# Seven products per pair of chunks: where the next pair's x is prepared, and when results are planted

## The chip, the core and the metric

One core of one Trainium2 chip runs the whole program: attention with landmarks, an MLP, a two-dimensional Fourier mix, a second MLP. The metric is the device time of one execution in microseconds (us); the core's engines are TensorE (PE, with its weight loads PEld), VectorE (DVE), ScalarE (ACT), GpSimd (POOL) and SyncE (SP), which issues the DMAs that matter here.

## The reference, cut to what matters

The change lies in the last stage: the second half of the second MLP.

```python
def _moe2_ref(x, w_ch1, w_ch2):
    X = np.fft.fft(x, axis=1)
    X = np.fft.fft(X, axis=2)
    mixed = np.real(X).astype(np.float32)
    u = x + mixed
    mu = np.mean(u, axis=-1, keepdims=True)
    var = np.mean((u - mu) ** 2, axis=-1, keepdims=True)
    un = (u - mu) / np.sqrt(var + 1e-06)
    ch = np.maximum(un @ w_ch1, 0.0) @ w_ch2
    return (u + ch).astype(np.float32)
```

`x` is 8 × 576 × 512, `w_ch1` 512 × 2048, `w_ch2` 2048 × 512, all float32.

## The kernel before, in words

The 4608 tokens are nine chunks of 512. Every float32 operand is kept as a high and a low part, and a product is three matmuls (high·high, low·high, high·low, each 128×128 times 128×512). The hidden 2048 columns are done in four quarters of 512; the last two are `quarters`, one pass over all chunks for each (`p` = 0, 1). A pass has five **units**: chunk 0 alone (the *single unit*), then four **pairs** of chunks. So there are ten units, numbered 0 to 9; 0 and 5 are the single ones.

In a pair the two chunks' up-projection is one 2 × 2 block product, made from seven block products instead of eight: sums and differences of blocks of x (`prepare`: `a` = x12 − x11, `b` = x22 − a, x12 ← x22 − x12, x21 ← x21 − b) meet blocks of weights that were combined beforehand, and partial sums in PSUM are copied on and added (`up_two`). The seven are the *roles* 0 to 6 of x: x11, a, b, x21, x12, x22, x21. The order of all work is written by hand: a unit is a list of **slots** (30 in a pair, 16 in a single unit), one slot is six matmuls of TensorE, `at(slot, fn)` files everything else. Each engine runs what it was given in the order of the slots, and within a slot in the order of filing: `up_two` or `up_one`, then `down`, then `prepare`, then loads.

- `up_two`, slots 0 to 13: two of the seven products' halves per role (lines 387 to 389). Line 494 (ACT) copies partial sums from bank to bank and the block s5 into SBUF; line 514 (DVE) makes the four **sums** (block c or b plus s5) in slots 8 to 11. `rectify`: line 455 (ACT) is the **Relu** into the high part of g, line 458 (DVE), a slot later, the **rest**, its low part.
- `down`, from slot 14 of a pair and slot 8 of a single unit: eight (four) result products of two slots each (lines 548 to 550). `get_res` (line 223, SP) fetches what earlier quarters left in DRAM, `plant` (line 539, ACT) copies it into the PSUM bank, where the product is added; only unit 0 adds it afterwards (line 555, DVE). The second pass also multiplies by a scale (559) and adds a skip (562). The four buffers `res` come free at the plant.
- `prepare` for the next unit, filed by this one: for each role `high` (line 421, ACT, the **cast**) and `low` (line 408, DVE, the **low**), and the **differences** (line 408, DVE too). Before, role r of a pair began in slot 2 + 3r, so 2, 5, 8, 11, 14, 17, 20.
- `load` (line 198, SP) for the unit after next: x11, x12, x22, x21 in slots 12, 22, 24, 27 of a pair; eight buffers `xf` in turn.

SP's queue is in order, and a DMA whose buffer is still read waits at its head. During the last pair of the first pass the eleven weights of the second pass (line 255, 512 KB each) pass through it too.

Of the kernel before, what the change touches and what calls it, by code (L numbers as in the profile page):

```python
# [34 lines left out]
def f32(ap):  # L35
    return ap.bitcast(F32)
# [3 lines left out]
def body(ctx: ExitStack, tc: tile.TileContext, qT, kT, vn, mU, mV, w11, w12, w21, w22,  # L40
# [146 lines left out]
    def rows(d):  # L187
        return slice(d * P, (d + 1) * P)
# [47 lines left out]
    class Mlp:  # L236
# [154 lines left out]
        def quarters(self, tail, ys, w1s, w2s, dst):  # L391
# [12 lines left out]
            def at(s, *fns):  # L404
                slots.add(s, [(0, fn) for fn in fns])

            def minus(out, a, b):
                nc.vector.tensor_tensor(out, a, b, op=ALU.subtract)

            def load(i, key):  # L410
                h, r = key
                c = units[i][1][h]
                ts = xin.setdefault(i, {})[key] = [self.pool.tile([P, NC], F32, name="xf", bufs=8) for _ in range(2)]
                for k in range(2):
                    un.get(c, 2 * r + k, ts[k])

            def high(i, r, k, src):
                n = 2 * r + k
                t = self.xtile(n)
                xs.setdefault(i, {})[r, k] = t  # L420
                nc.scalar.copy(t[:, 0, :], src())

            def low(i, r, k, src):
                t = xs[i][r, k]
                minus(t[:, 1, :], src(), f32(t[:, 0, :]))

            def prepare(i, s0, step):

                def X(h, r, k):
                    return lambda: xin[i][h, r][k]  # L430

                def sub(out, a, b):
                    return lambda: minus(out(), a(), b())

                pair = len(units[i][1]) == 2
                for k in range(2):
                    x11, x21 = X(0, 0, k), X(0, 1, k)
                    if pair:
                        x12, x22 = X(1, 0, k), X(1, 1, k)
                        a, b = (lambda k=k: t1[k]), (lambda k=k: t2[k])  # L440
                        pre = {1: [sub(a, x12, x11)], 2: [sub(b, x22, a)], 4: [sub(x12, x22, x12)], 6: [sub(x21, x21, b)]}
                        roles = (x11, a, b, x21, x12, x22, x21)
                    else:
                        pre = {2: [sub(x21, x21, x11)]}
                        roles = (x11, x21, x21)
                    for r, src in enumerate(roles):
                        s = s0 + step * r + k
                        at(max(s - 1, s0 + k) if r else s, *pre.get(r, ()))
                        at(s + 1, lambda r=r, k=k, src=src: high(i, r, k, src))
                        at(s + 2, lambda r=r, k=k, src=src: low(i, r, k, src))  # L450

            def rectify(g, key, src, s, wait=0):
                def relu():
# [64 lines left out]
            def down(i, s0, g):  # L518
                p, unit = units[i]
                seed = i > 0  # L520
                res, skip, sc, ps, out = {}, {}, {}, {}, {}
                outs = [(h, d) for h in reversed(range(len(unit))) for d in range(4)]

                def get_res(j, c, d):
                    res[j] = lp.tile([P, NC], F32, name="res", bufs=4)
                    ys[p].get(c, d, res[j])

                def get_skip(j, c, d):
                    skip[j] = lp.tile([P, NC], F32, name="skip", bufs=4)
                    tail[1].get(c, d, skip[j])  # L530

                def get_sc(c):
                    sc[c] = lp.tile([P, NC], F32, name="sc", bufs=2)
                    tail[0].get(c, sc[c])

                def plant(j):
                    ps[j] = self.bank8()
                    if seed:
                        nc.scalar.copy(ps[j], res[j])  # L539

                def mul(j, h, d, half):
                    w = self.w2[d]
                    ks = (2, 3, 0, 1) if h else (0, 1, 2, 3)
                    for k in ks[2 * half:2 * half + 2]:
                        gh, gl = g[h, k][:, 0, :], g[h, k][:, 1, :]
                        wh, wl = w[:, 0, rows(k)], w[:, 1, rows(k)]
                        first = not seed and k == ks[0]
                        nc.tensor.matmul(ps[j], wh, gh, start=first, stop=False, skip_group_check=True)  # L548
                        nc.tensor.matmul(ps[j], wl, gh, start=False, stop=False, skip_group_check=True)  # L549
                        nc.tensor.matmul(ps[j], wh, gl, start=False, stop=k == ks[3], skip_group_check=True)  # L550

                def take(j, c):
                    o = out[j] = lp.tile([P, NC], F32, name="out", bufs=3)
                    if not seed:
                        nc.vector.tensor_tensor(o, ps[j], res[j], op=ALU.add)
                    elif p == 0:
                        nc.scalar.copy(o, ps[j])
                    else:
                        nc.vector.tensor_tensor(o, ps[j], sc[c], op=ALU.mult)

                def add(j):
                    nc.vector.tensor_tensor(out[j], out[j], skip[j], op=ALU.add)

                def put(j, c, d):
                    dst[p].put(c, d, out[j])

                end = i + 1 == len(units)
                for j, (h, d) in enumerate(outs):
                    c, s = unit[h], s0 + 2 * j
                    lag = 0 if end and j + 1 == len(outs) else 1  # L570
                    at(max(s - 9, s0 - 8 + j), lambda j=j, c=c, d=d: get_res(j, c, d))
                    at(s - 3, lambda j=j: plant(j))
                    for half in range(2):
                        at(s + half, lambda j=j, h=h, d=d, half=half: mul(j, h, d, half))
                    at(s + 1, lambda j=j, c=c: take(j, c))
                    if p:
                        if d == 0:
                            at(s - 8, lambda c=c: get_sc(c))
                        at(max(s - 5, s0 - 6 + j), lambda j=j, c=c, d=d: get_skip(j, c, d))
                        at(s + 1 + lag, lambda j=j: add(j))  # L580
                    at(s + 1 + lag * (1 + p), lambda j=j, c=c, d=d: put(j, c, d))
# [14 lines left out]
            for i, (p, unit) in enumerate(units):  # L596
                s0, g, two = base[i], {}, len(unit) == 2
                last = unit == chunks[-1] and p == 0

                def begin(i=i, s0=s0, g=g, two=two, last=last):  # L600
                    (up_two if two else up_one)(i, s0, g)
                    down(i, s0 + (14 if two else 8), g)
                    if i + 1 < len(units):
                        prepare(i + 1, s0 + (2 if two or i else 6), 3 if two else 2)
                    if i + 2 < len(units):
                        for key, s in (((0, 0), 12), ((1, 0), 22), ((1, 1), 24), ((0, 1), 27)):
                            if key[0] < len(units[i + 2][1]):
                                at(s0 + (s if two else max(s - 12, 6)), lambda key=key: load(i + 2, key))
                    if last:
                        for n in range(7):  # L610
                            at(s0 + 2 * n + 3, lambda n=n: (self.w1.append(0), self.w1.pop(), self.fetch("w1", w1s[n])))
                        for d in range(4):
                            at(s0 + 24 + 2 * d, lambda d=d: self.fetch("w2", w2s[d]))
                for s in range(s0, s0 + lens[i]):
                    if s == s0:
                        if i and units[i - 1][0] != p:
                            self.w1, self.w2 = self.w1[7:], self.w2[4:]
                        begin()
                    slots.run(s)
                    yield 1  # L620
# [817 lines left out]
```

## Time and profile before

| | us |
|---|---|
| median of three runs | 1900.45 (1896.96 to 1901.38) |
| the profiled execution: time / span | 1895.0 / 1893.2 |
| TensorE busy | 1838.3 |
| VectorE / ScalarE / GpSimd busy | 1018.3 / 705.9 / 373.6 |
| mean granted clock of TensorE | 0.995 |

The span is from the first to the last instruction of the profiled execution. Times in the trace are us from its start. Busy time is a mean over stages, so each stage has to be looked at by itself. A wait is put down to the instruction that came last before it ended.

### The profile page before, as it was taken

Reading aid. Unit: us, or ns where it says so; the run is one execution under the profiler, and the core shown is the slowest. Engines: PE = TensorE matmul, PEld = TensorE weight load, DVE = VectorE, ACT = ScalarE, POOL = GpSimd, SP = SyncE. Lnnn points to the kernel's source line nnn. Section 1 sums busy time; section 2 is a strip of 40 time slices with the busy share of each in tenths; the row PEclk is TensorE's granted clock in tenths of the full one; section 3 lists DMA queues with packets and bytes.
Section 4 is the critical chain, followed back from the end, with each engine's and each line's share of the span. In section 5 each row is a group of like instructions: output and inputs, shape, how many; then the busy total and the mean of one; then the engine's idle time right before and its main releaser. Section 6 shows DMA issues by size and latency. Waiting matters only on the chain.

```text
span 1893.2 us, 30600 instructions
## 1 busy us (share of the span) xinstructions
PE 1838.3 (97%) x12088; PEld 1484.4 (78%) x12088; DVE 1018.3 (54%) x1764; ACT 705.9 (37%) x1469; POOL 373.6 (20%) x352
## 2 busy tenths in 40 slices
PE   6989999999999999999999999999999999999998
PEld 5767777777788888887887888888888877777777
DVE  7886556555323334755645455474332364438764
ACT  3544443444212212323333243343322365546442
POOL 2333211221201221313222043232321000000000
PEclk9999999999999999999999999999999999999999
DMA  7444445442537333524536554243533555476665
GB/s 262 143 171 159 146 165 199 140 154 99 179 126 272 126 130 117 171 95 156 191 106 244 173 178 160 90 155 120 164 104 113 178 178 150 134 250 207 207 188 156
DMA packets 175391, 305.56 MB, mean 161 GB/s; under 512 B 27440, under 2 KB 92560, under 8 KB 175248
## 3 DMA queue, kind: packets, MB, share of 16 engines
q1 hardware_dynamic: 170640, 294.17, 46.7%
q10 hardware_dynamic: 4608, 9.44, 1.3%
q8 instruction: 95, 1.56, 0.3%
q14 instruction: 48, 0.39, 0.1%
HBM read 195.74 MB, written 107.22 MB: 160 GB/s over the span
## 4 chain that ended last, share of the span: by engine, by line
PE 86%; DVE 7%; ACT 3%; DMA 3%; issue 1%; SPq 0%; ACTq 0%; POOL 0%; DVEq 0%
PE ps L348 10%; PE ps L350 10%; PE ps L349 10%; PE ps L299 10%; PE ps L301 9%; PE ps L300 9%; PE ps L548 4%; PE ps L550 3%; PE ps L549 3%; PE ps L389 2%; PE ps L388 2%; PE ps L387 2%; PE ps_f L76 1%; PE ps_f L77 1%; PE ps_f L78 1%
## 5 line engine op out<-in xcount | busy, mean ns | idle before, releaser
L299 PE MATMUL ps<-x,w 128*128 128x512 f32 x864 | 345.5, 400 | 0.0
L348 PE MATMUL ps<-g,w 128*128 128x512 f32 x864 | 345.4, 400 | 0.0
L350 PE MATMUL ps<-g,w 128*128 128x512 f32 x864 | 337.5, 391 | 0.9 <-DVE g L304 0.7
L301 PE MATMUL ps<-x,w 128*128 128x512 f32 x864 | 337.4, 390 | 0.0
L349 PE MATMUL ps<-g,w 128*128 128x512 f32 x864 | 337.0, 390 | 0.0
L300 PE MATMUL ps<-x,w 128*128 128x512 f32 x864 | 336.9, 390 | 0.0
L304 DVE SCALAR_TENSOR_TENSOR g<-ps,g 128x512 fp32r<-128x512 f32 x216 | 148.8, 690 | 333.0 <-ACT g L303 332.3
L303 ACT ACTIVATE g<-ps 128x512 fp32r<-128x512 f32 x216 | 128.9, 597 | 374.5 <-PE ps L301 373.8
L348 PEld LDWEIGHTS ps<-g,w 128*128 128x128 f32 x864 | 162.1, 188 | 39.2 <-issue 5.3
L350 PEld LDWEIGHTS ps<-g,w 128*128 128x128 f32 x864 | 162.2, 188 | 37.0 <-DVE g L304 2.1
L301 PEld LDWEIGHTS ps<-x,w 128*128 128x128 f32 x864 | 162.1, 188 | 35.1
L299 PEld LDWEIGHTS ps<-x,w 128*128 128x128 f32 x864 | 162.2, 188 | 34.4
L300 PEld LDWEIGHTS ps<-x,w 128*128 128x128 f32 x864 | 162.5, 188 | 31.6
L349 PEld LDWEIGHTS ps<-g,w 128*128 128x128 f32 x864 | 162.4, 188 | 31.5
L104 POOL TENSOR_TENSOR cvp<-cvp,cva 128x512 f32<-128x512 f32 x56 | 72.7, 1299 | 383.8 <-DVE cvp L103 383.8
L548 PE MATMUL ps<-g,w 128*128 128x512 f32 x288 | 115.6, 402 | 14.2 <-ACT ps L539 14.2
L358 DVE TENSOR_TENSOR xf<-ps,xf 128x512 f32<-128x512 f32 x76 | 52.4, 689 | 123.0 <-PE ps L350 121.0
L550 PE MATMUL ps<-g,w 128*128 128x512 f32 x288 | 114.8, 399 | 0.3 <-DVE g L458 0.3
L549 PE MATMUL ps<-g,w 128*128 128x512 f32 x288 | 114.8, 398 | 0.0
L52 POOL TENSOR_TENSOR x<-xf,x 128x512 fp32r<-128x512 f32 (+7 forms) x56 | 67.6, 1211 | 237.2 <-ACT x L51 218.3
L548 PEld LDWEIGHTS ps<-g,w 128*128 128x128 f32 x288 | 55.6, 193 | 29.5 <-ACT ps L539 17.9
L52 POOL TENSOR_TENSOR stg<-cva,stg 128x512 fp32r<-128x512 f32 x40 | 57.3, 1432 | 72.0 <-ACT stg L51 71.6
(350 smaller groups left out, 2886.5 us busy)
## 6 DMA issues: line engine op xcount, KB each, us to landing
d<-stg SPq DMA_DIRECT2D x54, 512.0 KB
w<-d SPq DMA_DIRECT2D x54, 512.0 KB
wraw<-w SPq DMA_DIRECT2D x48, 512.0 KB
y<-xf SPq DMA_DIRECT2D x76, 256.0 KB
res<-y SPq DMA_DIRECT2D x72, 256.0 KB
xf<-y SPq DMA_DIRECT2D x40, 256.0 KB
u<-u1T ACTq DMA_DIRECT2D x32, 288.0 KB
U<-x SPq DMA_DIRECT2D x8, 1152.0 KB
```

The lines of the kernel that those rows point to most:

```text
L52: (eng or nc.vector).tensor_tensor(lo, src, f32(hi), op=ALU.subtract)
L299: nc.tensor.matmul(ps, wh, xh, start=k == 0, stop=False)
L300: nc.tensor.matmul(ps, wl, xh, start=False, stop=False)
L301: nc.tensor.matmul(ps, wh, xl, start=False, stop=k == 3)
L303: nc.scalar.activation(g[:, 0, :], ps, AF.Relu)
L304: nc.vector.scalar_tensor_tensor(out=g[:, 1, :], in0=ps, scalar=0.0, in1=f32(g[:, 0, :]), op0=ALU.max, op1=ALU.subtract)
L348: nc.tensor.matmul(ps, wh, gh, start=k == m0, stop=False)
L349: nc.tensor.matmul(ps, wl, gh, start=False, stop=False)
L350: nc.tensor.matmul(ps, wh, gl, start=False, stop=k == m1 - 1)
L548: nc.tensor.matmul(ps[j], wh, gh, start=first, stop=False, skip_group_check=True)
L549: nc.tensor.matmul(ps[j], wl, gh, start=False, stop=False, skip_group_check=True)
L550: nc.tensor.matmul(ps[j], wh, gl, start=False, stop=k == ks[3], skip_group_check=True)
```

## The change

The slots of the preparation become a list: in a pair the roles begin in 2, 4, 13, 16, 19, 22, 25, so that no role lies in slots 8 to 13; the differences are filed behind the low of the role before. Results are planted at `s - 4` instead of `s - 3` and fetched at `s - 10` instead of `s - 9`. The loads stand in slots 10, 24, 27, 29 of a pair. The single units have lists of their own.

```diff
@@ def prepare @@
-            def prepare(i, s0, step):
+            def prepare(i, s0, starts):
...
-                        pre = {1: [sub(a, x12, x11)], 2: [sub(b, x22, a)], 4: [sub(x12, x22, x12)], 6: [sub(x21, x21, b)]}
+                        pre = {0: [sub(a, x12, x11)], 1: [sub(b, x22, a)], 3: [sub(x12, x22, x12)], 5: [sub(x21, x21, b)]}
                         roles = (x11, a, b, x21, x12, x22, x21)
                     else:
-                        pre = {2: [sub(x21, x21, x11)]}
+                        pre = {1: [sub(x21, x21, x11)]}
                         roles = (x11, x21, x21)
                     for r, src in enumerate(roles):
-                        s = s0 + step * r + k
-                        at(max(s - 1, s0 + k) if r else s, *pre.get(r, ()))
+                        s = s0 + starts[r] + k
                         at(s + 1, lambda r=r, k=k, src=src: high(i, r, k, src))
-                        at(s + 2, lambda r=r, k=k, src=src: low(i, r, k, src))
+                        at(s + 2, lambda r=r, k=k, src=src: low(i, r, k, src), *pre.get(r, ()))
@@ def down @@
-                    at(max(s - 9, s0 - 8 + j), lambda j=j, c=c, d=d: get_res(j, c, d))
-                    at(s - 3, lambda j=j: plant(j))
+                    at(max(s - 10, s0 - 8 + j), lambda j=j, c=c, d=d: get_res(j, c, d))
+                    at(s - 4, lambda j=j: plant(j))
@@ def quarters @@
-                        prepare(i + 1, s0 + (2 if two or i else 6), 3 if two else 2)
+                        prepare(i + 1, s0, (2, 4, 13, 16, 19, 22, 25) if two else range(2, 16, 2) if i else range(7, 21, 2))
                     if i + 2 < len(units):
-                        for key, s in (((0, 0), 12), ((1, 0), 22), ((1, 1), 24), ((0, 1), 27)):
+                        for key, s in (((0, 0), 10), ((1, 0), 24), ((1, 1), 27), ((0, 1), 29)):
+                            if not two:
+                                s = {10: 8, 24: 14, 27: 17, 29: 19}[s] + (5 if i == 0 else 0)
                             if key[0] < len(units[i + 2][1]):
-                                at(s0 + (s if two else max(s - 12, 6)), lambda key=key: load(i + 2, key))
+                                at(s0 + s, lambda key=key: load(i + 2, key))
```

The changed file has one line less above `rectify`, so its lines from there to the lists of loads are numbered one lower than before (457 for 458, 513 for 514, 538 for 539).

VectorE's queue in a pair, from the first sum to the last (w_14139 is the sum, w_14136 s5, w_14137 the block a, w_14138 the block b; ps is a PSUM bank). Before:

```order
L514 TENSOR_TENSOR w_14139<-ps,w_14136 128x512
L458 SCALAR_TENSOR_TENSOR g<-ps_14739,g 128x512
L408 TENSOR_TENSOR x<-w_14137,x 128x512
L408 TENSOR_TENSOR w_14138<-xf,w_14137 128x512
L458 SCALAR_TENSOR_TENSOR g<-w_14139,g 128x512
L514 TENSOR_TENSOR w_14139<-ps,w_14136 128x512
L514 TENSOR_TENSOR w_14139<-ps_14748,w_14136 128x512
L458 SCALAR_TENSOR_TENSOR g<-w_14139,g 128x512
L408 TENSOR_TENSOR xs<-w_14138,xs 128x512
L458 SCALAR_TENSOR_TENSOR g<-w_14139,g 128x512
L514 TENSOR_TENSOR w_14139<-ps_14749,w_14136 128x512
```

The same place in the change:

```order
L513 TENSOR_TENSOR w_14139<-ps,w_14136 128x512
L457 SCALAR_TENSOR_TENSOR g<-ps_14739,g 128x512
L457 SCALAR_TENSOR_TENSOR g<-w_14139,g 128x512
L513 TENSOR_TENSOR w_14139<-ps,w_14136 128x512
L513 TENSOR_TENSOR w_14139<-ps_14748,w_14136 128x512
L457 SCALAR_TENSOR_TENSOR g<-w_14139,g 128x512 x2
L513 TENSOR_TENSOR w_14139<-ps_14749,w_14136 128x512
L457 SCALAR_TENSOR_TENSOR g<-w_14139,g 128x512
```

The two lows and the difference that stood between the sums are gone from there.

ScalarE's queue in the single unit of the second pass, from its first two Relus on (the third Relu makes the first half of what the second of the unit's result slots reads). Before:

```order
L455 ACTIVATE g<-ps 128x512 x2
L421 CAST x<-xf 128x512 x2
L455 ACTIVATE g<-ps 128x512
L539 COPY ps_15842<-res 128x512
L421 CAST x<-w_14137 128x512 x2
L455 ACTIVATE g<-ps_15853 128x512
L539 COPY ps_15878<-res 128x512
```

In the change:

```order
L454 ACTIVATE g<-ps 128x512 x2
L421 CAST x<-xf 128x512
L538 COPY ps_15829<-res 128x512
L421 CAST x<-xf 128x512
L454 ACTIVATE g<-ps 128x512
L421 CAST x<-w_14137 128x512
L538 COPY ps_15859<-res 128x512
L421 CAST x<-w_14137 128x512
L454 ACTIVATE g<-ps_15852 128x512
```

The first plant has moved past one cast and the third Relu, the second past a cast and the fourth Relu.

SP's queue at the end of the pair ahead of that unit (w is a weight of the second pass, y a result written, xf a load of x in pieces of two batches, res the first result that the single unit plants). Before:

```order
L255 DMA w_15742<-d_19_172 128x1024
L198 DMA xf<-un_183 128x64
L198 DMA xf<-un_184 128x448
L198 DMA xf<-un_183 128x64
L198 DMA xf<-un_184 128x448
L226 DMA y_7_103<-out 128x512
L255 DMA w_15765<-d_20_173 128x1024
L226 DMA y_7_103<-out 128x512
L255 DMA w_15776<-d_21_174 128x1024
L223 DMA res<-y_0_96 128x512
```

In the change:

```order
L226 DMA y_7_103<-out 128x512
L255 DMA w_15759<-d_20_173 128x1024
L198 DMA xf<-un_183 128x64
L198 DMA xf<-un_184 128x448
L198 DMA xf<-un_183 128x64
L198 DMA xf<-un_184 128x448
L226 DMA y_7_103<-out 128x512
L255 DMA w_15776<-d_21_174 128x1024
L223 DMA res<-y_0_96 128x512
```

The last load of x has moved behind one more weight and one more written result, next to the first fetch of a result.

## Rows read from the trace of the kernel before

**Rows 1.** The page, busy time: engine, us, share of the span, instructions.

```profile
PE 1838.3 (97%) x12088; PEld 1484.4 (78%) x12088; DVE 1018.3 (54%) x1764; ACT 705.9 (37%) x1469; POOL 373.6 (20%) x352
```

**Rows 2.** TensorE in order of time: start, us, line, tiles [idle before, releaser].

```profile
1494.63 0.39 PE L387 MATMUL ps<-x,w 128*128 128x512 f32 x1
...
1505.29 0.39 PE L389 MATMUL ps<-xs,w 128*128 128x512 f32 x1
...
1537.58 0.63 PE L548 MATMUL ps<-g,w 128*128 128x512 f32 x1 [1.99 <-ACT ps L539]
...
1693.56 0.39 PE L387 MATMUL ps<-x,w 128*128 128x512 f32 x1
...
1707.58 0.50 PE L550 MATMUL ps<-g,w 128*128 128x512 f32 x1 [0.30 <-DVE g L458]
...
1888.21 0.39 PE L550 MATMUL ps<-g,w 128*128 128x512 f32 x1
```

**Rows 3.** Waits from 1494.6 to 1893.2: us in total, times, longest.

```profile
PE ps L548 <- ACT ps L539: 14.2, 8, 2.1
...
PE ps L550 <- DVE g L458: 0.3, 1, 0.3
```

**Rows 4.** Busy time, granted clock (PEclk), DMA share and GB/s behind two waits.

```profile
1537.60:1541.30 3.70, 3.70 (x9) 2.91 (x10) 3.39 (x7) 2.48 (x5) 0.00 (x0) 0.54 0.40 104
1582.20:1585.90 3.70, 3.70 (x16) 3.09 (x17) 3.39 (x7) 3.15 (x7) 0.00 (x0) 1.00 0.46 110
```

**Rows 5.** VectorE in order of time, unit 0 and the first pair.

```profile
1508.94 0.69 DVE L555 TENSOR_TENSOR out<-ps,res 128x512 f32<-128x512 f32 x1 [0.65 <-DMA res<-y]
...
1523.78 0.69 DVE L408 TENSOR_TENSOR w<-xf 128x512 f32<-128x512 f32 x1
...
1529.49 0.69 DVE L514 TENSOR_TENSOR w<-ps,w 128x512 f32<-128x512 f32 x1 [0.86 <-ACT ps L494]
1530.10 0.68 DVE L458 SCALAR_TENSOR_TENSOR g<-ps,g 128x512 fp32r<-128x512 f32 x1
...
1531.90 0.68 DVE L458 SCALAR_TENSOR_TENSOR g<-w,g 128x512 fp32r<-128x512 f32 x1
...
1535.69 0.68 DVE L514 TENSOR_TENSOR w<-ps,w 128x512 f32<-128x512 f32 x1
```

**Rows 6.** ScalarE in order of time, the first pair.

```profile
1530.22 0.63 ACT L455 ACTIVATE g<-w 128x512 fp32r<-128x512 f32 x1 [0.76 <-DVE w L514]
...
1536.41 0.63 ACT L455 ACTIVATE g<-w 128x512 fp32r<-128x512 f32 x1 [1.01 <-DVE w L514]
1536.95 0.58 ACT L539 COPY ps<-res 128x512 f32<-128x512 f32 x1
```

**Rows 7.** SP's own waits, 1494 to 1893: total, times, longest.

```profile
SPq L198 <- DVE xs L408: 18.0, 7, 7.1
```

**Rows 8.** SP's queue in order of time: start, us, line, tiles, DMAs.

```profile
1518.80 2.00 SPq L198 DMA_DIRECT2D xf<-un  x4
...
1683.95 1.83 SPq L198 DMA_DIRECT2D xf<-un  x4
...
1696.90 0.51 SPq L223 DMA_DIRECT2D res<-y  x1
...
1866.47 0.32 SPq L223 DMA_DIRECT2D res<-y  x1
```

**Rows 9.** ScalarE in order of time: two plants that waited for their result.

```profile
1703.85 0.59 ACT L539 COPY ps<-res 128x512 f32<-128x512 f32 x1 [1.33 <-DMA res<-y]
...
1869.82 0.59 ACT L539 COPY ps<-res 128x512 f32<-128x512 f32 x1 [0.84 <-DMA res<-y]
```

**Rows 10.** As rows 4, up to the first result of the second pass.

```profile
1684.00:1692.00 8.00, 8.00 (x37) 6.60 (x37) 0.00 (x0) 2.75 (x6) 0.00 (x0) 1.00 0.80 221
1692.00:1704.00 12.00, 12.00 (x55) 9.93 (x54) 4.99 (x8) 3.56 (x7) 0.00 (x0) 1.00 1.02 379
```

**Rows 11.** The page, DMA issues: queue, times, KB each.

```profile
w<-d SPq DMA_DIRECT2D x54, 512.0 KB
...
res<-y SPq DMA_DIRECT2D x72, 256.0 KB
```

## The prediction

> **What bounds the kernel now.** I first read the page's head: TensorE is busy for 97% of the span [rows 1], so time is to be won only where it stands or runs slowly. Then I took TensorE's instructions in order of time, and who waits for whom, in the part that the change touches. The diff touches only `quarters`, which runs from the first product of line 387 at 1494.63 to the last of line 550 at 1888.21 [rows 2]. It issues 1632 products (256 on each of lines 387 to 389, 288 on each of 548 to 550). The first 47 steps from one to the next take 10.66 us, from 1494.63 to 1505.29, so a step is 0.2268 us, and a slot of six 1.361 us. 1631 such steps are 369.9 us; the stretch is 393.6 us long. So **23.7 us** is all that can be won.
>
> Where they are: TensorE waited 14.2 us in eight waits on line 548 for ScalarE's line 539, and 0.3 us once for VectorE [rows 3]. The eight are the eight pair units, at the same place: the first result product (slot 14) stands until its planted result is there. Seven last 1.93 to 2.06 us, as at 1537.58 [rows 2]; the last pair, which prepares nothing, waits 0.32. From start to start each is 0.16 longer than its idle time, so the eight are 15.5 us. After four of them the granted clock went to its lower level, 1.2 GHz: 0.54 on average in the 3.7 us behind the first, with nine products done, while it was 1.00 behind the second, with sixteen [rows 4]. Such a stretch costs seven steps of 0.2268, 1.6 us, four of them 6.5. The rest is 0.6 in the single unit of the second pass, where line 550 at 1707.58 should by the same count have started at 1706.94 (1693.56 and 59 steps), and about 1 in steps of 0.1.
>
> Why ScalarE is late: in the first pair (its slot 14 is due at 1535.46, 30 slots after 1494.63) VectorE starts the first sum at 1529.49 and the last at 1535.69 [rows 5]; three of the instructions that stand between them are line 408, the preparation. The last Relu waits for that last sum and the plant stands behind this Relu in ScalarE's queue: 1536.41, 1536.95, ending 1537.53 [rows 6].
>
> **The change, part by part.** No instruction is added or dropped; all terms are waits.
>
> 1. *Preparation out of slots 8 to 13.* Between the first and the last sum VectorE's queue now holds rests and sums alone. I walk it with the spacings of the rows (0.60 for VectorE, 0.53 for ScalarE). Sum at 1529.49, rest 1530.10, first Relu of a sum 1530.22 as before [rows 6], done 1530.85; its rest 1530.9 instead of 1531.90 [rows 5]; the next two sums 1531.5 and 1532.1; their Relus 1532.2 and 1532.75.
>
> 2. *Plant a slot sooner.* It stands now behind the third Relu, not the fourth: start 1533.3, end 1533.9. Due at 1535.46, it has 1.6 us to spare. The third and second rests follow (1532.85, 1533.45), the fourth sum at 1534.05, its Relu at 1534.8, its rest at 1535.45, done at 1536.1; this one is due a slot after the plant, at 1536.8. So the wait goes in all seven, and in the last pair, 0.48 from start to start, too. The low stretches of the pairs all stood behind such waits and go with them: **15.5 + 6.5 + 1 = 23 us** go. The moved work fits: slots 4 to 7 get nine VectorE instructions of 0.60, 5.4 us of the 5.4 that four slots last, and the slots from 8 on, two each, are under 1.36.
>
> 3. *Loads behind the last use.* SP is one queue in order, and a load put before its buffer is free holds up all behind it: 18.0 us in seven waits, up to 7.1 [rows 7]. Now it doesn't stand there. Its price is less time from load to use: for x12 from 12 slots to 10, 13.6 us; for x22 from 13 to 9, 12.2 us. A transfer of 256 KB in a quiet stretch is ready 3.35 us after its issue (1866.47 to 1869.82 [rows 8, 9]); in the worst one that the rows show 6.95 (1696.90 to 1703.85 [rows 8, 9]). I count nothing. Bounds: none at 6.95; 0.5 for x12 if a wait of SP of 7.1 came before that as well (14.05 against 13.6).
>  In the first pair the distance is shortest: the load of x12 now stands in slot 19, its first use in slot 20. By VectorE's queue, 18 instructions after 1508.94 [rows 5] x12 is read for the last time, so the load starts at 1520.5 (1518.80 before [rows 8]); with 3.35 for its second half, issued 0.5 later, it is there at 1524.3. VectorE gets to its first reader 25 instructions after 1508.94, at 1524.0 (1523.78 before [rows 5]). 0.3 us of lateness against the 1.6 of point 2: nothing. With 6.95 it would be a wait of about 2 and a stretch of low clock, 0 to 3.7 us.
>
> 4. *The single unit of the second pass.* Here something new is late. Before, ScalarE stood until 1703.85 for the first result from DRAM [rows 9], but the Relu for half the next slot was already done. Planted a slot sooner, the plant stands **ahead** of one cast of x, of that Relu and of what they feed. Walked from the landing P: cast P+0.53, Relu P+1.05; then VectorE, in its new order, low, difference, rest, low, difference, low, difference, rest: eight at 0.60 from P+1.2, the last over at P+6.1. The last product of slot 9 needs that last rest. At the same landing this is 1709.95 instead of 1707.58, 2.4 us later. And the landing moves: the loads ahead of it start two slots (2.72 us) later, from the 1683.95 of before [rows 8], into DMA queues which were 0.80 busy for 8 us and then full, 1.02, up to the landing [rows 10]. At most 1.6 us of the 2.72 can be made good (0.20 of 8); I take half, 0.8, so the landing is 1.9 late. Sum 4.3 us, with 0.6 of before 4.9; and since four waits in seven of about 2 us brought the low clock, 1.6 more: **6.5 us** lost here. Bounds: 0 (three loads and four weights of 512 KB, four results of 256 KB and its own [rows 11] are 4.75 MB, at 379 GB/s [rows 10] 12.5 us; so it would land before its plant is due) to 7.4 (all of 2.72, and the low clock).
>
> Sum: 23.7 − 6.5 = **17.2 us**. The profiled execution took 1895.0, so 1877.8; it lies 5.45 under the median of 1900.45, from which the forecast goes: **1883 us**. A measurement of this kernel can tell some 0.3%, 5.7 us, from no change.
>
> **Rivals.** (a) *The single unit loses nothing*, since SP, no longer held up for the late plants of the pair before it, is through sooner. For: SP's loads stood in such waits [rows 7]. Against: the DMA queues, not SP, were full from 1692 on [rows 10]. 1900.45 − 23.7 + 0.6 = 1877.
>
> (b) *Pairs wait for DMA instead.* The plant is asked for at 1533.3, its result is issued in slot 6 of the pair, 1524.6: 8.7 us, a slot less than before, and a ScalarE that stands there holds the Relu behind it. Against: 6.95 was the worst landing. Two or three pairs at 2.1 + 1.6 give back 7 to 11 us: 1890 to 1894, with the first pair's wait of point 3 in the same sum.
>
> (c) *Slower: the later loads become the bound.* VectorE meets the first reader of x12 in slot 4, with the sums of slot 8 queued behind it. From 13.6 + 1.6 = 15.2 us after the issue on, each us of landing is one us of wait, in seven pairs, with 1.6 of low clock each. It must eat 17.2 + 5.7 = 23 us, so 3.3 per pair: landings of 17 us. Against: 6.95 is the longest in the rows; for: in the second pass the loads now stand within six slots, beside what the results move. It would give 1906 to 1915. The Trainium skill, "DMA: Bandwidth & Descriptors", section "Rules for kernel authors", says to issue a DMA early and wait for it late, which speaks for this rival; the trace agrees only so far as the buffer is free, since a load issued before that made SP stand up to 7.1 us [rows 7].
>
> (d) *No change*: the wait at slot 14 comes back from another side, say the fourth Relu's rest. Point 2 leaves it 0.7 us of room. 1900.
>
> **Chances.** Forecast 50% (own range 1879 to 1888: point 4 with at least 2 of its loss, points 3 and 4 at their upper bounds), (a) 25%, (b) 16%, (c) 4%, (d) 5%. (b) is faster by over 5.7 us in nearly all of its range; so faster 0.91, same 0.05, slower 0.04. The range leaves out (c), (d) and the upper end of (b), and reaches below (a) by the 3 us by which the runs of before spread under their median: 1874 to 1891.
>
> **What would show it.** Right: no wait of line 547 (548 before) for the plant in the eight pairs; clock 1.00 throughout them; rests and sums side by side on VectorE; in the single unit a wait of 2 us or more between its slots 8 and 10, ended by the plant or by VectorE. Wrong: waits of about 2 us still at slot 14, then the VectorE queue was not the cause; ScalarE standing for results from DRAM in the pairs, then (b); VectorE standing for x, then (c).

## The result and the profile after

The changed kernel takes **1878.86 us** (median of four runs, 1875.06 to 1879.98); the kernel before took 1898.70 beside it (four runs, 1896.90 to 1901.38). The ratio is 0.9891, with a 95% interval of 0.9870 to 0.9912: 19.8 us less. The forecast was 1883, range 1874 to 1891. Unrounded it was 1900.45 − 17.2 = 1883.25; of the 4.4 us between, 1.75 are the median of before, which a fourth run moved from 1900.45 to 1898.70, and 2.6 are one term of the sum.

The page of after, its busy line (all of after's lines behind `prepare` carry a number one lower than before's):

```profile
PE 1838.0 (98%) x12088; PEld 1486.0 (79%) x12088; DVE 1020.0 (54%) x1764; ACT 707.6 (38%) x1469; POOL 374.1 (20%) x352
```

Over the whole span the busy times are those of [rows 1] within 2 us. In the part that the diff touches TensorE's is not: the same products take longer at the lower clock. From the first product of line 387 on, before and after (busy time of each engine, then granted clock, DMA share and GB/s):

```profile
1494.63:1888.60 393.97, 379.47 (x1633) 309.90 (x1631) 228.71 (x362) 194.93 (x355) 0.00 (x0) 0.98 0.60 187
1499.38:1873.60 374.22, 371.54 (x1633) 305.81 (x1631) 230.66 (x362) 195.58 (x355) 0.00 (x0) 1.00 0.63 197
```

Of the gain there, 11.8 us are idle time that is gone (14.5 to 2.7), and 7.9 are busy time (379.5 to 371.5). TensorE's waits in the part (us in total, times, longest), against the 14.2 in eight of [rows 3]:

```profile
PE ps L549 <- DVE g L457: 2.0, 2, 1.7
PE ps L547 <- ACT ps L538: 0.5, 1, 0.5
```

These three are in the single unit of the second pass. No pair waits for its plant any more, and the granted clock stays at 1.00 behind every first result product of a pair.

A total needs care here. The code ahead of `quarters` is the same in all kernels, yet the first product of line 387 comes at 1494.63 in the profile of before and between 1496.57 and 1501.22 in the other nine. So I compare this **part** by itself, from the first product of line 387 to the last of line 549 (550): 393.58 us before, 373.81 after (1499.38 to 1873.19). The steps alone need 369.9; 23.7 us of excess have become 3.9. That saves 19.8, as the medians do.

**A pair after the change.** VectorE in the second pair, slots 8 to 12 (start, us, line, tiles):

```profile
1575.29 0.69 DVE L513 TENSOR_TENSOR w<-ps,w 128x512 f32<-128x512 f32 x1 [0.39 <-ACT ps L493]
1575.90 0.68 DVE L457 SCALAR_TENSOR_TENSOR g<-ps,g 128x512 fp32r<-128x512 f32 x1
1576.68 0.69 DVE L457 SCALAR_TENSOR_TENSOR g<-w,g 128x512 fp32r<-128x512 f32 x1
1577.29 1.28 DVE L513 TENSOR_TENSOR w<-ps,w 128x512 f32<-128x512 f32 x2
1578.67 1.29 DVE L457 SCALAR_TENSOR_TENSOR g<-w,g 128x512 fp32r<-128x512 f32 x2
1579.88 0.68 DVE L513 TENSOR_TENSOR w<-ps,w 128x512 f32<-128x512 f32 x1
```

Four sums and four rests, and no line 408 between them. The same pair on ScalarE (the second and third Relu of a sum, then the plant), and its first result product on TensorE:

```profile
1578.01 1.23 ACT L454 ACTIVATE g<-w 128x512 fp32r<-128x512 f32 x2 [0.88 <-DVE w L513]
1579.14 0.58 ACT L538 COPY ps<-res 128x512 f32<-128x512 f32 x1
```

```profile
1581.29 0.39 PE L547 MATMUL ps<-g,w 128*128 128x512 f32 x1
```

The plant stands behind three Relus, not four, and ends at 1579.72, 1.57 us before it is needed. Point 2 gave it 1.6.

**The single unit of the second pass**, where 3.7 of the 3.9 us are. Its first product is at 1684.65. SP issues the fetch of its first result, ScalarE plants it, VectorE makes what follows, TensorE waits three times:

```profile
1690.08 0.45 SPq L223 DMA_DIRECT2D res<-y  x1
```

```profile
1695.58 0.59 ACT L538 COPY ps<-res 128x512 f32<-128x512 f32 x1 [4.18 <-DMA res<-y]
1696.10 0.61 ACT L421 CAST x<-xf 128x512 fp32r<-128x512 f32 x1
1696.62 0.59 ACT L454 ACTIVATE g<-ps 128x512 fp32r<-128x512 f32 x1
```

```profile
1696.75 0.69 DVE L408 TENSOR_TENSOR x<-xf,x 128x512 fp32r<-128x512 f32 x1 [3.94 <-ACT x L421]
...
1700.96 0.68 DVE L457 SCALAR_TENSOR_TENSOR g<-ps,g 128x512 fp32r<-128x512 f32 x1
```

```profile
1696.22 0.50 PE L547 MATMUL ps<-g,w 128*128 128x512 f32 x1 [0.53 <-ACT ps L538]
...
1698.70 0.51 PE L549 MATMUL ps<-g,w 128*128 128x512 f32 x1 [0.37 <-DVE g L457]
...
1701.70 0.50 PE L549 MATMUL ps<-g,w 128*128 128x512 f32 x1 [1.66 <-DVE g L457]
```

ScalarE stands 4.18 us at the plant, and the cast and the Relu behind it hand the delay on. The last product of slot 9 comes 6.12 us behind the landing (the prediction walked 6.1). By 59 steps it was due at 1698.03; 3.67 are lost.

### The profile page after: what moved, and what is told of

The parts are those of the page before. It is cut to its first block, busy times and chain, and to the rows that moved or that the text cites. A ratio compares the mean times of both kernels' runs of the same rounds, so it can differ in the third digit from the quotient of the medians.

```text
span 1878.2 us, 30591 instructions
## 1 busy us (share of the span) xinstructions
PE 1838.0 (98%) x12088; PEld 1486.0 (79%) x12088; DVE 1020.0 (54%) x1764; ACT 707.6 (38%) x1469; POOL 374.1 (20%) x352
## 4 chain that ended last, share of the span: by engine, by line
PE 89%; DVE 4%; DMA 4%; ACT 2%; issue 1%; SPq 0%; POOL 0%; ACTq 0%; DVEq 0%
PE ps L348 10%; PE ps L350 10%; PE ps L349 10%; PE ps L299 10%; PE ps L301 9%; PE ps L300 9%; PE ps L547 3%; PE ps L549 3%; PE ps L548 3%; PE ps L387 3%; PE ps L388 3%; PE ps L389 3%; DMA U<-x 1%; PE ps_f L76 1%; PE ps_f L77 1%; PE ps_f L78 1%
## 5 line engine op out<-in xcount | busy, mean ns | idle before, releaser
L348 PEld LDWEIGHTS ps<-g,w 128*128 128x128 f32 x864 | 162.4, 188 | 39.4 <-issue 5.3
L350 PEld LDWEIGHTS ps<-g,w 128*128 128x128 f32 x864 | 162.6, 188 | 37.8 <-DVE g L304 2.9
L349 PEld LDWEIGHTS ps<-g,w 128*128 128x128 f32 x864 | 162.8, 188 | 31.8
L101 ACT ACTIVATE wraw<-wraw 128x512 f32<-128x512 f32 x48 | 32.6, 678 | 91.2 <-DVE cva L97 89.8
```

Of the source, the lines that this page charges most:

```text
L348: nc.tensor.matmul(ps, wh, gh, start=k == m0, stop=False)
L349: nc.tensor.matmul(ps, wl, gh, start=False, stop=False)
L350: nc.tensor.matmul(ps, wh, gl, start=False, stop=k == m1 - 1)
```

## The experiments

Each ran beside the kernel before: the first four share a median of 1897.57 of it (seven runs), the others 1898.14 (fifteen runs). The ratios on record are not exactly the quotients of these medians. "Part" is the stretch defined above, "excess" what it lasts over 369.9.

| run | median, us | ratio (95%) | part | excess |
|---|---|---|---|---|
| before | 1897.57; 1898.14 | | 393.58 | 23.7 |
| plant_only | 1877.00 | 0.9891 (0.9873 to 0.9909) | 371.91 | 2.0 |
| prep_only | 1885.01 | 0.9931 (0.9915 to 0.9946) | 378.27 | 8.4 |
| late_single | 1876.48 | 0.9883 (0.9866 to 0.9900) | 372.20 | 2.3 |
| early_loads | 1875.46 | 0.9883 (0.9868 to 0.9897) | 370.13 | 0.2 |
| old_loads | 1876.55 | 0.9889 (0.9865 to 0.9912) | 372.81 | 2.9 |
| plant_late | 1902.16 | 1.0016 (1.0004 to 1.0028) | 394.75 | 24.8 |
| early_loads_5 | 1875.70 | 0.9875 (0.9858 to 0.9893) | 370.48 | 0.6 |
| change_again | 1878.72 | 0.9893 (0.9877 to 0.9909) | 373.55 | 3.6 |

**The plant and the fetch alone** (before, with two numbers changed):

```diff
-                    at(max(s - 9, s0 - 8 + j), lambda j=j, c=c, d=d: get_res(j, c, d))
-                    at(s - 3, lambda j=j: plant(j))
+                    at(max(s - 10, s0 - 8 + j), lambda j=j, c=c, d=d: get_res(j, c, d))
+                    at(s - 4, lambda j=j: plant(j))
```

> The plants and fetches of the change, with the preparation and the loads as before. Theory 1 (the plant stands behind the fourth Relu, which waits for a VectorE queue with line 408 between the sums): one Relu less ahead of the plant takes it from 1536.95 to about 1534.8 in the first pair of before, 0.6 us ahead of the product's due time, so the eight waits shrink to 0 to 0.3 us each although VectorE's queue is as crowded as before, and the low clock goes with them; the single unit of the second pass waits 2 to 3 us. 19 to 21 us less than before: 1878 to 1880. Theory 2 (only the crowded VectorE queue matters): waits of 1 to 1.5 us stay in the seven pairs, 1887 to 1891.

Measured 20.6 us less than before: the whole gain, with the preparation and the loads where they were. TensorE's waits in the part, then ScalarE and the first result product of the second pair:

```profile
PE ps L550 <- DVE g L458: 0.5, 1, 0.5
PE ps L548 <- ACT g L455: 0.2, 1, 0.2
```

```profile
1581.69 0.63 ACT L455 ACTIVATE g<-w 128x512 fp32r<-128x512 f32 x1
1582.23 0.57 ACT L539 COPY ps<-res 128x512 f32<-128x512 f32 x1
```

```profile
1582.92 0.44 PE L548 MATMUL ps<-g,w 128*128 128x512 f32 x1
```

The sums are as late as ever, but the plant no longer stands behind the last of them. It ends at 1582.80, 0.12 before it is needed (0.05 in the first pair): just enough. ScalarE never stood for a DMA at the first plant of a pair, in this run or before, so it is the plant that did this and not the fetch that moved with it. Theory 1 holds, but for the single unit, which lost 1.1 us and not 2 to 3. What the moved preparation buys in a pair is 1.45 us of reserve (1.57 against 0.12). Little of it is used: of the 2.0 of excess left here, some 0.8 lie in the pairs, 0.08 to 0.18 in each of seven.

**The preparation and the loads alone** (the change, with the plant and the fetch put back):

```diff
-                    at(max(s - 10, s0 - 8 + j), lambda j=j, c=c, d=d: get_res(j, c, d))
-                    at(s - 4, lambda j=j: plant(j))
+                    at(max(s - 9, s0 - 8 + j), lambda j=j, c=c, d=d: get_res(j, c, d))
+                    at(s - 3, lambda j=j: plant(j))
```

> The preparation and the loads of the change, with plants and fetches as before. Theory 1: the fourth sum comes some 1.6 us sooner, its Relu starts about 0.6 us ahead of the first result product and the plant behind it is 0.4 to 0.5 us late, as in the last pair of before, which prepares nothing: eight waits of 0.3 to 0.5 us, no low clock behind them, the single unit as before at 0.6 to 1.5: 17 to 19 us less than before, 1880 to 1882. Theory 2: no waits, 1876 to 1878. Theory 3 (the plant's slot alone matters): waits of about 2 us stay, 1895 to 1899.

Measured 12.6 us less by the medians, 15.3 by the part; the two differ by about as much as the stretch ahead of the part does between profiles. The wait does not quite go:

```profile
PE ps L547 <- ACT ps L538: 4.7, 9, 1.3
PE ps L549 <- DVE g L457: 0.9, 1, 0.9
```

Of the nine, 1.33 is the first pair, 0.90 the single unit, and the other seven are 0.32 to 0.38, what the last pair of before showed, which prepares nothing (0.32). That is the price of the fourth Relu ahead of the plant by itself. The first pair's 1.0 more comes with the moved preparation: its first sum starts 14.05 us behind the pair's first product (13.04 to 13.10 in the other pairs, and 13.10 in this pair of before); old_loads, which has the preparation moved and the loads of before, has it late as well (14.23). Theory 1 had the waits of the seven pairs right and its time too low, for the 1.0 of the first pair and for 2.2 in the single unit instead of 0.6 to 1.5. The two parts overlap: 20.6 and 12.6 us alone, 19.8 together.

**A plant a slot later** (before, the opposite way), to see the same cause doubled:

```diff
-                    at(s - 3, lambda j=j: plant(j))
+                    at(s - 2, lambda j=j: plant(j))
```

> The kernel before with the plants a slot later instead of sooner; fetches as before. Theory 1 (the wait is the plant's place in ScalarE's queue): the plant now stands behind one Relu more, 0.5 us, so the seven waits of 1.93 to 2.06 become 2.4 to 2.6 and that of the last pair 0.8. If the low clock depends on how long TensorE stood, it follows more of the seven than the four of before, at 1.6 us each: 4 to 9 us slower than before, 1902 to 1907. Theory 2 (the low clock falls by chance): again three to five of seven, 1901 to 1904.

Measured 4.0 us more than before (ten runs; by the interval of the ratio 0.8 to 5.3). The eight waits, two of them on TensorE, and the clock behind these two (columns as in [rows 4]):

```profile
PE ps L548 <- ACT ps L539: 18.1, 8, 2.5
```

```profile
1541.07 0.80 PE L548 MATMUL ps<-g,w 128*128 128x512 f32 x1 [2.47 <-ACT ps L539]
...
1740.07 0.50 PE L548 MATMUL ps<-g,w 128*128 128x512 f32 x1 [2.47 <-ACT ps L539]
```

```profile
1541.10:1544.80 3.70, 3.70 (x10) 2.98 (x11) 3.36 (x6) 1.95 (x4) 0.00 (x0) 0.61 0.38 105
...
1740.10:1743.80 3.70, 3.70 (x16) 3.09 (x17) 3.48 (x7) 3.08 (x7) 0.00 (x0) 1.00 0.62 165
```

Seven waits last 2.42 to 2.54, the last 0.81: each 0.48 to 0.49 longer than before, 3.9 us in all. In the profile the part grew by 1.2 alone, because the low clock fell once less than in before and the single unit lost nothing. ScalarE has one more Relu between the fourth and the plant, as in the first pair:

```profile
1539.41 0.63 ACT L455 ACTIVATE g<-w 128x512 fp32r<-128x512 f32 x1 [1.01 <-DVE w L514]
1539.95 0.58 ACT L455 ACTIVATE g<-ps 128x512 fp32r<-128x512 f32 x1
1540.42 0.59 ACT L539 COPY ps<-res 128x512 f32<-128x512 f32 x1
```

With the two runs above, the wait at slot 14 is shown to be the plant's place in ScalarE's queue. The clock fell behind three of the seven, where before it was four: in these two profiles longer waits did not bring it more often, and the measured time lies in the ranges of both theories.

**The plant of the single units put back** (the change, with one exception):

```diff
-                    at(s - 4, lambda j=j: plant(j))
+                    at(s - 4 if len(unit) == 2 else s - 3, lambda j=j: plant(j))
```

> The change, with the plants of the two single units a slot later, as before; fetches as in the change. Theory 1 (the new wait of 3.7 us in the single unit of the second pass is the chain behind the plant: cast, Relu, two VectorE instructions, rest, then four more and the last rest): the third Relu is done before the landing, the last rest ends 4.3 us after it instead of 6.1, so 1.8 us less wait, 1877. Theory 2 (the wait is the landing alone): no difference in the wait, 1879.

Measured excess 2.3 us instead of 3.6 to 3.9. The plant, and TensorE's two waits:

```profile
1697.58 0.59 ACT L538 COPY ps<-res 128x512 f32<-128x512 f32 x1 [2.44 <-DMA res<-y]
```

```profile
1698.22 0.50 PE L547 MATMUL ps<-g,w 128*128 128x512 f32 x1 [1.00 <-ACT ps L538]
...
1701.90 0.50 PE L549 MATMUL ps<-g,w 128*128 128x512 f32 x1 [0.90 <-DVE g L457]
```

The chain behind the landing is 4.32 us (1697.58 to 1701.90) instead of 6.12, since one cast, one Relu and three of VectorE's instructions are done before the result lands. But the landing was the latest of all runs, 11.40 behind the unit's first product, so only 1.3 was won.

**Earlier loads in the last pair of the first pass** (the change, and in that pair alone three loads 8 or 9 slots sooner):

```diff
                             if not two:
                                 s = {10: 8, 24: 14, 27: 17, 29: 19}[s] + (5 if i == 0 else 0)
+                            elif last:
+                                s = {10: 10, 24: 16, 27: 18, 29: 20}[s]
```

> The change, with the three later loads of x in the last pair of the first pass in slots 16, 18, 20 instead of 24, 27, 29 (their buffers are free by then). Theory 1 (the first result of the single unit lands late because the loads of x fill the DMA queues ahead of it): it lands 4 to 6 us sooner, less than 7 us after the unit's first product instead of 10.9; the waits of that unit go from 3.7 us to under 0.7; 1875 to 1876. Theory 2 (weights and written results, or SP, set the landing): it lands within 1.5 us of where it did, the waits stay over 2 us, 1878 to 1879.

Measured excess 0.2 us; the list of TensorE's waits in the part is empty. SP's last load and its fetch, the plant, and the product that had waited 1.66:

```profile
1672.81 1.92 SPq L198 DMA_DIRECT2D xf<-un  x4
...
1685.89 0.43 SPq L223 DMA_DIRECT2D res<-y  x1
```

```profile
1691.72 0.59 ACT L538 COPY ps<-res 128x512 f32<-128x512 f32 x1 [0.79 <-DMA res<-y]
```

```profile
1697.85 0.50 PE L549 MATMUL ps<-g,w 128*128 128x512 f32 x1
```

The unit begins at 1684.18, so the landing is at 7.54, 3.4 sooner than in the change; the run was to show 4 to 6. The product that had waited 1.66 is 0.3 behind its due time. Theory 1 was right on the time but not on the cause: from its issue to its landing the result takes 5.83 here and 5.50 in the change. A fetch that SP issues 1.71 behind the unit's first product instead of 5.43 is what did it. The Trainium skill, "DMA: Bandwidth & Descriptors", section "Rules for kernel authors", says to issue a DMA early and wait for it late; this run agrees with 3.4 us of landing, by moving the transfers *ahead* of the one that is awaited.

Repeated, beside the change itself:

> The change with the last three loads of the first pass's last pair in slots 16, 18, 20, once more with more rounds beside the change itself: waits of 0.3 us in all against 3.7, so 3 to 3.5 us less than the change if TensorE's waits are all that differs; nothing, if what is won there is given back at the end.

> The change itself on the same chip: 3 to 3.5 us over the version with early loads, its waits in the single unit of the second pass 3 to 4.5 us, with low clock behind them in fewer than half of the profiles.

Measured 1875.70 (1874.89 to 1876.53) and 1878.72 (1877.68 to 1880.47) on the same chip: the ranges do not touch, the medians differ by 3.0 us, the parts by 3.1. The intervals of the two ratios overlap, so the order rests on these and on TensorE's waits (0.5 us on line 549 in early_loads_5; in change_again 0.6 and 2.0, as in the change). Against plant_only (1874.04 to 1879.85) early_loads cannot be told apart by its total.

**The loads of before** (the change, with the old load slots):

```diff
-                        for key, s in (((0, 0), 10), ((1, 0), 24), ((1, 1), 27), ((0, 1), 29)):
+                        for key, s in (((0, 0), 12), ((1, 0), 22), ((1, 1), 24), ((0, 1), 27)):
                             if not two:
-                                s = {10: 8, 24: 14, 27: 17, 29: 19}[s] + (5 if i == 0 else 0)
+                                s = max(s - 12, 6)
```

> The change with the loads of x in the slots of before. Theory 1 (the loads' part of the change wins nothing in itself; it only sets how late the single unit's first result lands): SP's waits for the preparation are back (20 us and more in all), no product of the pairs waits, the first result of the single unit lands 9.5 to 10.3 us after the unit's first product (10.9 in the change) and its waits, the landing plus 6.1 less 13.4, are 2.2 to 3.0 us instead of 3.7: 1877 to 1879. Theory 2 (the later loads are needed, because SP held up delays the results to be planted): ScalarE waits for results in the pairs and the products of slot 14 wait 0.5 us or more each; 1881 or more.

Measured 1876.55, excess 2.9. The single unit loses 2.1 instead of 3.7, because its first result is fetched sooner and lands at 9.30. SP's waits for buffers, then a wait of TensorE that no other run has, in the first pair of the second pass, and ScalarE ahead of it:

```profile
SPq L198 <- DVE xs L408: 28.7, 18, 8.4
```

```profile
1711.69 0.50 PE L387 MATMUL ps<-xs,w 128*128 128x512 f32 x1 [0.62 <-ACT ps L493]
```

```profile
1710.53 0.62 ACT L421 CAST xs<-xf 128x512 fp32r<-128x512 f32 x1 [3.27 <-DVE xf L408]
1711.06 1.06 ACT L493 COPY ps<-ps 128x512 f32<-128x512 f32 x2
```

SP stood 28.7 us in 18 waits, and no pair waited at its slot 14. The 0.62 comes from the longest of these waits. SP stood 8.4 us at a load whose buffer VectorE still read, with the write of a finished result (line 202, ready at 1699.39) behind it, and VectorE waited for that write, because with three `out` buffers the fourth result goes into the first one's:

```profile
1703.63 1.99 SPq L198 DMA_DIRECT2D xf<-un  x4
1705.66 0.43 SPq L202 DMA_DIRECT2D outT<-out  x1
```

```profile
1708.61 0.69 DVE L558 TENSOR_TENSOR out<-ps,sc 128x512 f32<-128x512 f32 x1 [2.01 <-DMA outT<-out]
```

VectorE's difference, the cast, the copy and TensorE's product are late one behind the other; the unit loses 0.9. So the moved loads win 0.9 us in this pair and lose 1.6 in the single unit. Theory 1 holds but for this wait; landing and loss are a little under its ranges.

**One account of the single unit, for all runs.** Fetch issued and result landed (the plant starts) are counted from its first product; the chain is the time from there to the last product of slot 9, which is due at 13.38 (59 steps). The loss is landing + chain − 13.38:

| run | issued | landed | chain behind it | loss |
|---|---|---|---|---|
| before | 3.34 | 10.29 | 3.73 | 0.6 |
| plant_only | 3.66 | 9.51 | 4.92 | 1.1 |
| prep_only | 5.28 | 11.29 | 4.33 | 2.2 |
| late_single | 5.71 | 11.40 | 4.32 | 2.3 |
| change | 5.43 | 10.93 | 6.12 | 3.7 |
| old_loads | 3.49 | 9.30 | 6.13 | 2.1 |
| early_loads | 1.71 | 7.54 | 6.13 | 0.3 |
| early_loads_5 | 1.71 | 7.86 | 6.13 | 0.6 |
| change_again | 5.16 | 10.97 | 6.13 | 3.7 |
| plant_late | 3.36 | by 9.57 | 3.80 | 0 |

In plant_late ScalarE comes to the plant at 9.57 and finds the result there.

From issue to landing it is 5.5 to 6.2 in every run but before (6.95), where it can be seen. What differs is when SP gets to the fetch: the load slots set that (3.3 to 3.7 with those of before, 5.2 to 5.7 with the change's, 1.7 with the early ones), and the slot of the fetch itself does not (plant_only has the change's, prep_only that of before). What stands behind the plant sets the chain.

## Why the prediction was right, and where it was off

The mechanism was forecast rightly, and the measured time alone doesn't show it. 1878.86 lies in the stated range, but that range was drawn to hold rival (a) too; it lies just under the forecast's own 1879 to 1888, and nearer to the 1877 of (a) than to 1883. That the forecast came about and not (a) is seen in the trace: the single unit lost 3.67 us, and (a) said that it would lose nothing.

*What bounds the kernel.* Right: 23.7 us were to be won in the part, and early_loads wins all but 0.2 of them.

*Point 1, the sums.* Right on VectorE: sums and rests side by side. For the time it was hardly needed, as plant_only shows (0.8 us in the pairs). The prediction gave the first 23 us to points 1 and 2 together and did not ask what either gives alone; [rows 6] show ScalarE idle for 1.01 us ahead of the fourth Relu, which is where a plant had room at once.

*Point 2, the plant.* Right: seven waits of 1.9 to 2.1 and the eighth of 0.32 gone, with 1.57 to spare against 1.6, and the stretches at 1.2 GHz with them. prep_only tests the other half of its arithmetic: with the plant left behind the fourth Relu, the Relu at 1534.8 would have put the plant's end at about 1535.9 against a due time of 1535.46, 0.45 late; 0.48 to 0.54 from start to start was measured in seven pairs.

*Point 3, the loads.* Counted as nothing. SP's waits for xs fell, as claimed, from the 18.0 of [rows 7] to

```profile
SPq L198 <- DVE xs L408: 4.1, 6, 2.6
```

and old_loads, with 28.7, shows what that is worth: 0.9 in one pair, nothing at slot 14 of any. In the change's first pair the plant is just too late, by 0.25 us between the products:

```profile
1539.70 0.58 ACT L538 COPY ps<-res 128x512 f32<-128x512 f32 x1
```

```profile
1540.33 0.50 PE L547 MATMUL ps<-g,w 128*128 128x512 f32 x1
```

This is not the late x12 for which point 3 gave 0 to 3.7: no idle time of VectorE in that preparation ends with a load of x. What it stood for is ahead of the preparation in its queue, the first result that unit 0 adds (line 554). The change, and the same kernel in change_again:

```profile
1514.18 0.69 DVE L554 TENSOR_TENSOR out<-ps,res 128x512 f32<-128x512 f32 x1 [2.34 <-DMA res<-y]
```

```profile
1511.31 0.69 DVE L554 TENSOR_TENSOR out<-ps,res 128x512 f32<-128x512 f32 x1 [1.49 <-DMA res<-y]
```

That is 14.80 and 13.94 us behind the first product of the pass. VectorE then starts the pair's first sum 4.3 us ahead of slot 14's due time in the change and 5.0 in change_again (6.0 in the other pairs), and in change_again the plant is 0.56 early and nothing is lost. So the 0.25 is one profile's late landing, on top of the 1.0 us of reserve that the moved preparation costs in this pair. The prediction has no term for either: it counted VectorE's instructions from the landing of before.

*Point 4, the single unit.* The mechanism is right: landing, ScalarE, a cast, a Relu, eight instructions of VectorE, 6.12 for 6.1. The term was mis-sized: **6.5 us forecast, 3.67 measured** (about 3.6 in the repetition, by the part). Two steps of it failed. "So the landing is 1.9 late": it was 0.64 later (10.93 against 10.29). The loads made the fetch 2.09 later on SP (5.43 against 3.34, not 2.72), and the transfer itself gave back 1.45 (5.50 against 6.95), where I had let it give back 0.8 of at most 1.6. And "1.6 more" for the low clock: it did not come. The windows up to the plant and behind the wait of 1.66:

```profile
1684.00:1696.00 12.00, 11.69 (x52) 9.36 (x50) 2.58 (x4) 2.72 (x5) 0.00 (x0) 1.00 1.01 350
1701.70:1705.40 3.70, 3.70 (x16) 3.09 (x17) 3.70 (x7) 1.60 (x5) 0.00 (x0) 1.00 0.16 59
```

The rule behind the 1.6, four of seven waits of about 2 us, was a frequency and not a certainty; a wait of 1.66 brought no low clock in any of three profiles. 1.26 of landing and 1.6 of clock are the 2.8 by which the term was too large; the sum would have been 23.7 − 3.7 − 0.25 = 19.8. (A slip in its lower bound: 4.75 MB counted in KB of 1024 take 13.1 us at 379 GB/s, not 12.5; nothing hangs on it.)

*The rivals.* (a), that the single unit loses nothing, did not happen, but my ground against it was wrong: "the DMA queues, not SP, were full". They were full (1.01, 350 GB/s), and still SP's queue decided, as the table shows: from issue to landing hardly varies, the issue does. With the loads out of SP's way (a) comes true. (b) and (c) did not happen: where the plant had its new slot, no product of a pair waited for a result from DRAM or for x, beyond the 0.25 above and the 0.62 of old_loads, where SP held a write. The sign that the prediction gave for (b), ScalarE standing for results in the pairs, was there, but it cost nothing: behind the first plant of pairs of the second pass ScalarE stood up to 2.46 us for a result, before up to 2.56, and TensorE did not wait. (d) fell with the waits.

## What to carry to other kernels

When an instruction is late in an in-order queue, look first at what stands ahead of it there: moving it past one instruction it does not need (two numbers) won 20.6 us, more than thinning out the work on another engine (12.6). Move an instruction that waits for a DMA ahead of others only where the landing is safe, because it hands its wait to all behind it. And keep the issuing queue clear ahead of the one transfer that is awaited next; transfers with time to spare go where nothing is due.

## What the runs showed that I had not expected

The low clock does not go by the length of a wait alone. In before, the granted clock fell to the level of 1.2 GHz behind four of seven waits of 1.93 to 2.06 us (those of 1.99, 1.99, 1.99 and 2.06, not those of 1.93, 1.93 and one of 1.99). In plant_late it fell behind three of seven of 2.42 to 2.54, each of them 2.47, and not behind a fourth of 2.47, nor behind 2.54. It never fell behind 1.66 (change, change_again, old_loads) or 1.33 (prep_only). What decides between waits of one length stays open.

In the last 45 us ahead of the single unit's first fetch the four DMAs of one load took SP 1.80 to 2.12 us in some places and 2.51 to 3.06 in others. Full DMA engines alone do not decide it: the same load took 1.92 in early_loads (1672.81, DMA share 1.07) and 2.90 in early_loads_5 (1671.48, share 0.99). What makes the difference stays open.
